# Attention and a gated FFN on one core: the list that sets the order of all steps, replaced

## The chip, the core and the metric

The kernel runs on one NeuronCore of a Trainium2 chip. Its engines are TensorE (PE for its matmuls, PEld for its weight loads), VectorE (DVE), ScalarE (ACT), GpSimd (POOL) and SyncE (SP), whose queue issues the DMAs here. The metric is the device time of one launch in microseconds; lower is better.

## The reference

```python
# q, k, v: (8 batches, 8 heads, 576 positions, 64)
scores = scale * np.matmul(q, k.transpose(0, 1, 3, 2))
rel = pos[:, None] - pos[None, :]
mask_plain = (rel >= 0) & (rel < 32)
mask_dil = (rel >= 0) & (rel < 128) & (rel % 4 == 0)       # heads 4 to 7
attn = softmax(np.where(masks, scores, -1e9))
x = np.matmul(attn, v).transpose(0, 2, 1, 3).reshape(4608, 512)
h = x @ w_in                                               # 512 x 2048
g = h * np.tanh(np.log1p(np.exp(np.minimum(h, 20.0))))     # h where h > 20
out = g @ w_out                                            # 2048 x 512
```

Attention looks back over 32 positions, plain in heads 0 to 3 and every fourth position in heads 4 to 7. The FFN is a product, the Mish function and a second product.

## The kernel before

**Units.** The work is cut into 16 units: half of one batch's positions, 288 each. A unit has four head pairs. Pairs 0 and 1 are plain heads (queries in blocks of 96 rows), pairs 2 and 3 are dilated ones (blocks of 72 rows, one for each residue). For units 0 to 3 attention runs in fp32 on TensorE; from unit 4 on q, k and v are split into two fp16 halves, and transposes go by DMA. The FFN of every unit is made of fp16 products with the high and low halves of weights and activations: 192 matmuls of 128 x 288 in each of the two layers.

**Steps.** The kernel is written as small generator functions, one for each step, and a list called ORDER names them one after another. Each appearance of a name runs the function to its next `yield`. So the list sets the order of the instructions on every engine, and an engine takes its instructions in that order. The steps that matter here, with the lines of the profile:

- `ld`, `lv`: DMAs of a unit's q and k, and of its v (L416 to L444).
- `sp`: the score products of a head pair. Two products with the mask `m_fb` come first (L593), then those of q and k (L596). `sc`: the maxima on DVE (L626). `ex`: for unit 0 TensorE subtracts the maxima (L648), then ACT takes the exponentials (L654); other units have them in L661 or L665.
- `tp`: transposes of the probabilities (L715), copied by ACT (L724). `va`: products with v (L738), the denominator on ACT (L752), the division on DVE (L758, L759).
- `tx`: transposes of the attention's result (L786, L789), its high half by ACT (L796), and its low half, for some pairs by TensorE and ACT (L799, L801).
- `pr`: the power-of-two scales of a unit's inputs, which take a maximum over all partitions (L299 to L308, L470).
- Weights: `wl` fetches a piece of w_in or w_out of 1 MB (L322, L324; 16 pieces, four buffers called `raw`), `wm` takes a copy on ACT (L337), `ww` joins the words of the 64-bit numbers on DVE (L380, L382, L383), `ws` sums over partitions on TensorE (L348, L351) and makes a scale from the maximum on DVE (L355 on), `wp` splits the weights into halves on ACT (L392) and DVE (L395). The first digit is the layer, the second a group of 512 columns, the third one of its two pieces.
- `ff`: products of the first layer (L840) and Mish on ACT (L843). `gt`: the gate's halves on ACT (L859) and DVE (L861). `fo`: products of the second layer (L871), the result (L885), and its DMA (L887).
- `kw`: so many products of zeros on TensorE (L900), whose result is never read. `kw16=0` is 16 of them into bank 0.

The number behind `=` is the buffer that a step takes: of the four PSUM banks, each a pair of 2 KB rows, and of a few SBUF buffers. A step that writes a bank waits until the last reader of it is done, and that holds for the products of zeros too.

```python
def keep_warm(n):
    warm = take("b", banks)
    for _ in range(n):
        nc.tensor.matmul(warm[:, 1, 512 - P:], zeros, zeros, start=True, stop=True)
...
for name in ORDER:
    name, _, at = name.partition("=")
    place[:] = [int(at)] if at else []
    ...
    if hasattr(begun[name], "__next__"):
        next(begun[name], None)
```

**Outside the list.** GpSimd makes an identity (`ident`) and the masks (`m_f`, L239 to L248) with its selection instructions at the kernel's start. ACT makes `ident_b`, `m_fb` and `minus` from them (L252, L250, L271), and the first score product reads `ident_b` and `m_fb`.

Of the kernel before, what the change touches and what calls it, by code (L numbers as in the profile page):

```python
# [42 lines left out]
kw10=3 tx0.2 tx0.2 va0.0 va0.0 tx0.3=3 tx0.3 kw16=0 kw7=0 tx0.3 tx0.3 va0.1=0 va0.1 va0.1 sp1.2=1 sc1.2 ex1.1 kw3=3
tp1.1=3 wl0.1.0 wm0.1.0 sp1.0=2 sc1.0 wl0.2.0 wm0.2.0 ww0.2.0 tx0.0=0 tx0.0 kw12=1 tx0.0 tx0.0 ex1.2 ww0.1.0 ww0.1.0
tx0.1=1 tx0.1 kw16=0 kw7=0 tx0.1 tx0.1 wl0.1.1 wm0.1.1 ww0.1.1 wl0.2.1 wm0.2.1 ww0.2.1 tp1.2=0 tp1.2 tp1.1 ld2 sp2.0=1
sc2.0 ex2.0 kw16=0 ws0.1=0 ex1.0 ww0.2.1 ws0.1 wp0.1.0 sp1.3=3 sc1.3 ex1.3 ww0.1.1 wp0.1.1 kw16=1 kw6=1 ws0.2=1 ws0.2
fs0 wp0.2.1 ff0.0=0 ff0.0 ff0.0 ff0.1=2 ff0.1 ff0.1 ff0.6=1 ff0.6 ff0.6 ff0.7=3 wp0.1.0 ww0.2.0 wp0.2.0 ff0.7 ff0.7
gt0.3=0 wp0.1.1 lv1 pr1 kw16=0 kw7=0 pr1=0 pr1 kw6=2 pr1 pr1 va1.1=2 va1.1 va1.1 va1.2=1 va1.2 va1.2 fs1 tp1.3=3 tp1.3
lv2 tp1.0=0 tp1.0 pr2 wl1.2.0 xa1 tx1.1=2 tx1.1 kw4=1 va1.3=1 va1.3 tx1.1 tx1.2=3 va1.0=0 tx1.2 va1.0 va1.0 va1.3
kw2=2 tx1.2 tx1.2 kw11=2 tx1.0=2 tx1.0 wp0.2.0 wl1.3.1 wm1.3.1 gt0.3 sp2.3=0 sc2.3 tx1.0 tx1.0 sp2.1=3 sc2.1 wl1.3.0  # L50
tx1.3=1 tx1.3 kw13=2 tx1.3 tx1.3 ff1.0=2 ff1.0 wp0.2.1 ex2.3 pr2=1 pr2 kw8=0 pr2 pr2 wm1.3.0 ex2.1 ff1.0 kw4=1 ff0.2=1
ff0.2 ff0.2 ww1.3.1 ff1.1=0 ff1.1 ff1.1 ww1.3.1 ww1.3.0 ww1.3.0 ws1.3=3 ws1.3 wm1.2.0 ww1.2.0 ww1.2.0 gt0.0=1 ff0.3=2
gt0.0 wl1.2.1 wm1.2.1 tp2.1=1 tp2.1 wp1.3.1 wp1.3.1 ff0.4=0 ff0.5=3 ff0.5 ff0.5 ff0.4 ff0.4 gt0.2=2 ww1.2.1 ww1.2.1
va2.1=1 va2.1 va2.1 tp2.3=3 tp2.3 ff0.3 xa3 ff0.3 gt0.1=3 gt1.0=4 wl1.1.0 ws1.2=0 ws1.2 wp1.2.1 wp1.2.1 gt1.0 wp1.3.0
wp1.3.0 gt0.2 ff1.2=3 ff1.3=2 ff1.3 ff1.2 ff1.2 ff1.3 gt1.1=5 gt1.1 va2.3=1 wp1.2.0 wp1.2.0 va2.3 ff1.4=0 ff1.4 ff1.4
fs2 ff1.5=3 va2.3 ff1.5 ff1.5 ld3 lv3 sp3.1=2 sc3.1 sp3.0=0 sc3.0 wm1.1.0 wl1.0.1 wm1.0.1 ww1.0.1 gt1.2=6 gt1.2 gt0.1
ff1.6=3 ff1.6 ff1.6 wl1.1.1 wm1.1.1 sp3.2=1 ww1.1.0 tp2.0=2 tp2.0 wl1.0.0 wm1.0.0 ww1.0.0 xa2 tx2.3=0 tx2.3 tx2.3
ww1.0.0 ff1.7=3 ff1.7 ff1.7 gt1.3=7 gt1.3 xa4 fo1.2.0=2 fo1.2.1 fo1.2.2 ww1.1.1 ex3.1 tp3.1=3 tp3.1 ws1.0=0 ws1.0
fo1.2.3 fo1.2.3 fo1.2.3 sc3.2 ex3.2 sp2.2=3 ld4 sc2.2 ex2.2 ww1.1.0 ex3.0 ws1.1=0 fo1.3.0 fo1.3.1 fo1.3.2 fo1.3.3
fo1.3.3 ws1.1 pr4 pr4 sp3.3=1 sc3.3 ex3.3 pr3 lv4 fo0.2.0=0 fo0.2.1 fo0.2.2 fo0.2.3 fo0.2.3 fo0.2.3 pr4 pr4 va2.0=3  # L60
tp2.2=2 tp2.2 va2.0 va2.0 wp1.0.0 wp1.0.0 fo0.3.0 fo0.3.1 fo0.3.2 fo0.3.3 fo0.3.3 pr4=1 ww1.0.1 fo1.3.3 pr4 fo0.3.3
tx2.0=2 va2.2=3 tx2.0 va2.2 tx2.0 pr4 pr4 tp3.0=0 tp3.0 pr3=2 pr3 va2.2 fo0.0.0=1 wp1.0.1 tx2.1=0 tx2.1 pr3 pr3
va3.1=3 va3.1 va3.1 tp3.2=2 tp3.2 fs4 fo0.0.1 tx2.1 tx2.1 wp1.0.1 tx3.1=2 va3.0=3 va3.0 va3.0 tp3.3=0 tp3.3 tx3.1
tx3.1 fo0.0.2 tx2.2=3 tx2.2 va3.3=0 va3.3 va3.3 tx2.2 tx2.2 ff2.0=2 tx3.3=3 tx3.3 ff2.0 ff2.0 tx3.3 tx3.3 fo0.0.3
fo0.0.3 fo0.0.3 ff2.1=0 ff2.1 ff2.1 ww1.1.1 wp1.1.1 wp1.1.1 va3.2=2 va3.2 va3.2 ff2.2=3 ff2.2 ff2.2 ff2.3=0 ff2.3
wp1.1.0 wp1.1.0 fo0.1.0 ol mr pr4 pr4 fo0.1.1 fo0.1.2 gt2.0=1 gt2.0 fo0.1.3 fo0.1.3 pr4 pr4 pr4 ld5 pr4 pr4 lv5 ff2.3
gt2.1=3 gt2.1 pr5 ff2.4=2 ff2.4 ff2.5=3 ff2.5 ff2.5 ff2.4 gt2.2=2 gt2.2 tx3.0=1 tx3.0 tx3.0 ff2.6=0 ff2.6 ff2.6
ff2.7=3 fo0.1.3 tx3.2=2 tx3.2 tx3.2 ff2.7 ff2.7 gt2.3=0 gt2.3 fo2.2.0=0 fo2.2.1 sp4.3=1 sc4.3 sp4.1=2 sc4.1 fo2.0.0=3
fo2.0.1 fo2.0.2 fs3 ff3.0=1 ff3.2=2 ff3.0 ff3.0 fo2.0.3 fo2.0.3 fo2.0.3 pr5 pr5 pr5 pr5=1 fo2.2.2 fo2.2.3 fo2.2.3 pr5
pr5 pr5 fo2.1.0 fo2.1.1 fo2.1.2 fo2.1.3 pr5 pr5 pr5 pr5 pr5 pr5 pr5 ld6 lv6 ff3.2 ff3.2 fo2.2.3 sp5.1=1 sc5.1 fo2.1.3  # L70
fo2.3.0 fo2.3.1 fo2.3.2 fo2.3.3 fo2.3.3 ex4.1 fo2.1.3 pr6 pr6 pr6 pr6 pr6 pr6 fo2.3.3 sp4.2=2 sc4.2 xa6 ex4.3 tp4.3=1
tp4.3 tp4.3=1 sp5.2=1 fo1.0.0=3 fo1.0.1 fo1.0.2 fo1.0.3 fo1.0.3 fo1.0.3 sp4.0=0 sc4.0 ex4.0 tp4.0=2 tp4.0 tp4.0=2
sc5.2 ff3.1=2 ff3.1 ff3.1 gt3.0=1 gt3.0 fo1.1.0 fo1.1.1 fo1.1.2 fo1.1.3 fo1.1.3 fo1.1.3 pr6 pr6 pr6 pr6 pr6 ld7 pr7
ff3.4=0 ff3.5=2 ff3.5 ff3.5 ff3.4 ff3.4 gt3.2=3 gt3.2 ff3.6=1 ff3.6 ff3.6 ff3.7=3 ff3.7 ff3.7 gt3.3=2 gt3.3 va4.0=2
# [884 lines left out]
```

## Time and profile before

| what | us |
|---|---|
| runs of the kernel before | 929.4, 934.27, 936.63 (median 934.27) |
| the profiled execution's own time | 933.42 |
| its span, first to last instruction | 931.6 |
| TensorE busy in the span | 911.0 |
| VectorE, ScalarE, GpSimd busy | 592.3, 541.0, 22.6 |
| products of zeros: number and busy time | 345, 25.7 |
| first-layer and second-layer products: number and busy time | 3072, 387.8 and 3072, 388.3 |

A row of the timeline has the start in us, the duration, the engine, the line, the operation, what it writes and reads, how many instructions are taken together, and in brackets the idle time of its engine just before it with what ended it. A row of the table by stretch has the stretch, its length, the busy time of PE, PEld, DVE, ACT and POOL with their counts, the clock that TensorE was granted (1.00 is full), the share of the DMA engines, and GB/s. A row of waits has the engine and line that waited, for whom, the us in total, how many times, and the longest.

### The profile page before, as it was taken

The numbers are of one execution on the slowest core, as the hardware profiler recorded it, in microseconds if no ns is written. First come the engines' busy times: TensorE is split into PE (matmuls) and PEld (weight loads), VectorE is DVE, ScalarE is ACT, GpSimd is POOL, SyncE is SP. The second block draws the span as 40 slices with busy tenths as digits, with TensorE's granted clock in tenths as the row PEclk, the third lists the DMA queues.
The fourth block names the chain that finished last, engine by engine and source line by source line (L and its number), as shares of the span: only waits on it lengthen the run. The fifth ranks groups of instructions, "written<-read, shape, count | busy, mean of one in ns | idle before, by whom it ended". The sixth has DMA issues, their size and how long they took to land.

```text
span 931.6 us, 21552 instructions
## 1 busy us (share of the span) xinstructions
PE 911.0 (98%) x9285; PEld 735.0 (79%) x9285; DVE 592.3 (64%) x879; ACT 541.0 (58%) x800; POOL 22.6 (2%) x99
## 2 busy tenths in 40 slices
PE   6889999999999999999999999999999999999998
PEld 4778788888778878878878888887888788788776
DVE  2877888647767767786958677766556757422020
ACT  1677785473566576666665676747545656653141
POOL 1000000040000000000000000000000000000000
PEclk6899999999999999999999999999999999999999
DMA  8283293003334344443434423453224432311000
GB/s 272 87 255 95 93 274 87 20 19 93 107 98 81 90 93 66 90 121 90 113 85 97 101 51 80 88 125 81 40 55 74 122 59 55 43 33 40 20 13 26
DMA packets 156558, 82.33 MB, mean 88 GB/s; under 512 B 122960, under 2 KB 152368, under 8 KB 156464
## 3 DMA queue, kind: packets, MB, share of 16 engines
q1 hardware_dynamic: 156464, 80.97, 34.9%
q8 instruction: 72, 1.18, 0.5%
q14 instruction: 22, 0.18, 0.1%
HBM read 49.02 MB, written 9.44 MB: 63 GB/s over the span
## 4 chain that ended last, share of the span: by engine, by line
PE 96%; issue 1%; ACT 1%; DVE 1%; POOL 0%; DVEq 0%; ACTq 0%; POOLq 0%
PE b L871 41%; PE b L840 40%; PE b L596 4%; PE b L744 3%; PE b L900 2%; PE b L738 2%; PE b L648 1%; PE b L715 1%; PE b L593 1%; PE b L351 0%; PE b L348 0%; PE b L786 0%; PE b L799 0%; ACT x L801 0%; PE b L308 0%
## 5 line engine op out<-in xcount | busy, mean ns | idle before, releaser
L871 PE MATMUL b<-g,w 128*128 128x288 f16 x3072 | 388.3, 286 | 0.0
L840 PE MATMUL b<-x,w 128*128 128x288 f16 x3072 | 387.8, 286 | 0.0
L840 PEld LDWEIGHTS <-w 128*128 128x128 f16 x3072 | 297.9, 98 | 75.8 <-issue 0.3
L871 PEld LDWEIGHTS <-w 128*128 128x128 f16 x3072 | 297.2, 98 | 74.9
L843 ACT ACTIVATE hm<-b,fs 128x576 f32<-128x576 f32 x128 | 92.9, 737 | 116.7 <-PE b L840 99.3
L861 DVE SCALAR_TENSOR_TENSOR g<-hm,sg,g 128x1152 f16<-128x1152 f32 x64 | 90.1, 1414 | 108.7 <-ACT g L859 108.7
L885 ACT ACTIVATE y<-b,fo 128x288 f32<-128x288 f32 x60 | 43.1, 722 | 110.1 <-PE b L871 102.7
L859 ACT ACTIVATE g<-hm,sg 128x1152 f16<-128x1152 f32 x64 | 79.8, 1253 | 3.1 <-PE b L871 1.6
L667 ACT ACTIVATE sb<-sb,ln_p 96x704 f32<-96x704 f32 (+3 forms) x48 | 42.2, 886 | 33.9 <-DVE sb L628 33.8
L628 DVE TENSOR_TENSOR sb<-sb,nm 72x576 f32<-72x576 f32 (+4 forms) x60 | 45.3, 754 | 2.1
L626 DVE TENSOR_REDUCE nm<-sb 72x8 f32<-72x576 f32 (+4 forms) x60 | 44.9, 748 | 1.6
L759 DVE TENSOR_TENSOR xs<-b,rec 96x384 f32<-96x384 f32 (+1 forms) x64 | 39.7, 620 | 6.4 <-DVE rec L758 0.5
L705 DVE TENSOR_TENSOR p<-sb,p 96x704 f16<-96x704 f32 (+3 forms) x31 | 27.7, 897 | 15.6 <-ACT p L703 15.4
L758 DVE RECIPROCAL rec<-den 96x6 f32<-96x6 f32 (+1 forms) x64 | 12.0, 188 | 38.5 <-ACT den L754 29.1
L900 PE MATMUL b<-zeros 128*128 128x128 f16 x345 | 25.7, 235 | 8.1 <-ACT pp L724 2.8
L596 PEld LDWEIGHTS <-q 64*72 64x72 f16 (+1 forms) x1008 | 25.7, 116 | 8.1 <-issue 7.4
L620 DVE SCALAR_TENSOR_TENSOR sb<-b,sc,m_d 72x576 f32<-72x576 f32 (+1 forms) x24 | 22.7, 944 | 14.7 <-PE b L596 11.4
L520 DVE TENSOR_TENSOR q<-qn,q 128x288 f16<-128x288 f32 (+1 forms) x36 | 23.4, 701 | 13.3 <-ACT q L511 13.3
L900 PEld LDWEIGHTS <-zeros 128*128 128x128 f16 x345 | 23.6, 107 | 10.5 <-issue 8.0
L620 DVE SCALAR_TENSOR_TENSOR sb<-b,sc,m_r 96x704 f32<-96x704 f32 (+1 forms) x24 | 23.4, 976 | 12.0 <-PE b L596 11.9
L596 PE MATMUL b<-k,q 64*96 64x128 f16 (+3 forms) x1008 | 30.7, 210 | 0.0
L626 DVE TENSOR_REDUCE nm<-b 96x4 f32<-96x512 f32 (+4 forms) x20 | 14.7, 749 | 20.3 <-PE b L596 20.3
(141 smaller groups left out, 837.9 us busy)
## 6 DMA issues: line engine op xcount, KB each, us to landing
qn<-in_qT SPq DMA_DIRECT2D x16, 576.0 KB
out_T<-y SPq DMA_DIRECT2D x64, 144.0 KB
raw<-in_w_in SPq DMA_DIRECT2D x16, 512.0 KB
raw<-in_w_out SPq DMA_DIRECT2D x16, 512.0 KB
vn<-in_v SPq DMA_DIRECT2D x48, 128.0 KB
knd<-in_kdT SPq DMA_DIRECT2D x16, 208.0 KB
vdn<-in_vd SPq DMA_DIRECT2D x32, 104.0 KB
knp<-in_kT SPq DMA_DIRECT2D x8, 320.0 KB
```

Of the source, the lines that this page charges most:

```text
L596: nc.tensor.matmul(o, q, k, start=start, stop=stop, skip_group_check=True)
L620: nc.vector.scalar_tensor_tensor(args[0], args[1], d["sc"][:nq], args[2], ALU.mult, ALU.add)
L626: nc.vector.tensor_reduce(nm[:nq, :, j:j + n], x, axis=AX.X, op=ALU.max, negate=True)
L628: nc.vector.tensor_tensor(blocked(sb, c0, n, w), x, nm[:nq, :, j:j + n].unsqueeze(3).broadcast_to([nq, 2, n, w]), op=ALU.add)
L667: nc.scalar.activation(x, x, AF.Exp, bias=ln_p[:nq])
L840: nc.tensor.matmul(ph[:, h, :HT], w1[j][:, c, wi, k * P:(k + 1) * P], x_of(d, xi, c), start=(n == 0), stop=(n == len(seq) - 1))
L843: nc.scalar.activation(d["m"][j][:, k0:k0 + 2], ph[:, :, :HT], AF.Mish, scale=d["fs"][:, j:j + 1])
L859: nc.scalar.activation(g[:, 0], m, AF.Identity, scale=sg)
L861: nc.vector.scalar_tensor_tensor(g[:, 1], m, sg, g[:, 0], ALU.mult, ALU.subtract)
L871: nc.tensor.matmul(po[:, :HT], w2[:, e, j, wi, k * P:(k + 1) * P], d["g"][j][:, gi, k, :], start=(j == 0 and n == 0), stop=(j == NCH - 1 a ...
L885: nc.scalar.activation(o, src, AF.Identity, scale=fo)
L900: nc.tensor.matmul(warm[:, 1, 512 - P:], zeros, zeros, start=True, stop=True)
```

## The change

The list ORDER is another one; no function is touched. The steps in it are the same, each as often as before, but for the products of zeros: 482 in place of 345. The list has one line more, so every line of the code behind it has a number that is higher by one.

Three stretches of it have another sequence of steps: from the beginning to the first steps of unit 2's first layer, a block that holds the second layer of unit 6 up to the attention of unit 12, and a few names between. All the rest keeps its sequence and has other bank numbers. Its beginning, as a diff:

```diff
-ld0 kw16=0 kw16=0 kw3=0 sp0.1=0 sp0.2=1 sc0.1 sc0.2 sp0.0=2 sc0.0 sp0.3=3 sc0.3 wl0.3.0 wm0.3.0 ex0.2 ww0.3.0 ww0.3.0
...
+wl0.3.0 wl0.0.1 ld0 wm0.3.0 ww0.3.0 ww0.3.0 wm0.0.1 ww0.0.1 ww0.0.1 kw16=0 kw16=0 kw16=0 kw16=0 kw16=0 kw16=0 kw16=0
+kw16=0 kw16=0 kw16=0 kw16=0 kw16=0 kw16=0 kw16=0 kw2=0 sp0.0=0 sc0.0 sp0.1=1 sc0.1 wl0.0.0 wm0.0.0 ww0.0.0 sp0.3=2
...
```

So 226 products of zeros stand ahead of the first score, where 35 stood, and the other 256 stand in 23 groups up to unit 2, where 310 stood in 20.

**The DMAs at the start.** These are SP's first rows, before; `raw` is a piece of w_in, `qn`, `knp` and `knd` are unit 0's q and k, `vn` and `vdn` its v:

```order
L416 DMA qn_127<-in_qT 128x1152
L418 DMA knp_129<-in_kT 128x2x288
L421 DMA knd_131<-in_kdT 128x4x72 x2
L322 DMA raw_215<-in_w_in 128x512 x2
L322 DMA raw_224<-in_w_in 128x512 x2
L442 DMA vn_293<-in_v 128x4x64 x3
L444 DMA vdn_294<-in_vd 72x4x64 x4
```

And now:

```order
L323 DMA raw_127<-in_w_in 128x512 x2
L323 DMA raw_130<-in_w_in 128x512 x2
L417 DMA qn_133<-in_qT 128x1152
L419 DMA knp_135<-in_kT 128x2x288
L422 DMA knd_137<-in_kdT 128x4x72 x2
L323 DMA raw_396<-in_w_in 128x512 x2
L323 DMA raw_411<-in_w_in 128x512 x2
```

Two pieces of the weights went ahead of q and k, and the next two ahead of v.

**ACT and DVE at the start.** ACT's first rows and DVE's, after three memsets, before; `w13` and `w10` are parts of the first layer's weights, `nm` the maxima of scores:

```order
L252 CAST ident_b_96<-ident_74 96x96
L250 ACTIVATE m_fb_94<-m_f_79 96x352
L271 ACTIVATE minus_100<-ident_74 128x128
L337 ACTIVATE w13_105<-raw_215 128x1024
L337 ACTIVATE w13_105<-raw_224 128x1024
L626 TENSOR_REDUCE nm_187<-b0_70 96x2x2
L626 TENSOR_REDUCE nm_190<-b1_71 72x8
L380 TENSOR_SCALAR w13_105<-w13_105 128x1024
```

And now:

```order
L338 ACTIVATE w13_105<-raw_127 128x1024
L253 CAST ident_b_96<-ident_74 96x96
L272 ACTIVATE minus_100<-ident_74 128x128
L338 ACTIVATE w10_102<-raw_130 128x1024
L251 ACTIVATE m_fb_94<-m_f_79 96x352
L381 TENSOR_SCALAR w13_105<-w13_105 128x1024
L383 SCALAR_TENSOR_TENSOR raw_127<-raw_127,w13_105 128x1024
L384 SCALAR_TENSOR_TENSOR raw_127<-raw_127 128x1024
L381 TENSOR_SCALAR w10_102<-w10_102 128x1024
L383 SCALAR_TENSOR_TENSOR raw_130<-raw_130,w10_102 128x1024
L384 SCALAR_TENSOR_TENSOR raw_130<-raw_130 128x1024
L627 TENSOR_REDUCE nm_382<-b0_70 96x2x2
```

ACT copies one piece ahead of `ident_b` and one ahead of `m_fb`; DVE joins the words of both pieces before its first maxima, where it had four pairs' maxima first.

**TensorE between the second sum of weights and unit 0's first `tx`.** Before, with the groups of zeros left out (`pp` are the transposed probabilities, `xs` the attention's result, the 96 x 384 products those of unit 1 with the mask):

```order
L348 MATMUL b2_72<-w10_102,ones_111 128x512
...
L738 MATMUL b3_73<-vdn_294,pp_390 72x65 x8
L715 MATMUL b1_71<-ident_74,sb_354 72x72 x8
...
L738 MATMUL b2_72<-vdn_294,pp_445 72x65 x8
...
L593 MATMUL b1_71<-m_fb_94,ident_b_96 96x384
...
L596 MATMUL b1_71<-knp_428,qn_426 96x128 x6
L786 MATMUL b0_70<-ident_74,xs_472 128x72 x4
```

And now:

```order
L349 MATMUL b1_71<-w10_102,ones_111 128x512
...
L594 MATMUL b3_73<-m_fb_94,ident_b_96 96x384
...
L597 MATMUL b3_73<-knp_571,qn_569 96x128 x6
...
L597 MATMUL b2_72<-knp_571,qn_569 96x128 x6
L739 MATMUL b1_71<-vdn_459,pp_528 72x65 x8
L716 MATMUL b0_70<-ident_74,sb_530 72x72 x8
...
L739 MATMUL b0_70<-vdn_459,pp_642 72x65 x8
...
L787 MATMUL b3_73<-ident_74,xs_622 128x72 x4
```

Two score pairs of unit 1 stand right behind the sum of weights, ahead of unit 0's products with v, where one stood behind them and the other further down.

More of the change, by code (lines that the diff above doesn't have):

```diff
@@ L43 @@
[L43 to L62, printed above, removed]
@@ new lines @@
+wp0.0.1 wp0.3.0 wp0.0.1 ld1 sp1.1=3 sc1.1 sp1.0=2 sc1.0 ex0.0 lv1 wp0.3.1 va0.2=1 kw11=0 tp0.3=0 tp0.3 va0.2 va0.2
+wp0.0.0 wp0.0.0 kw16=0 kw8=0 va0.3=0 va0.3 tp0.0=3 tp0.0 va0.3 ex1.0 wp0.3.1 wl0.1.0 wm0.1.0 ww0.1.0 ww0.1.0 wl0.2.1
+xa0 kw16=3 kw7=3 tx0.2=3 va0.0=1 tx0.2 kw15=2 tp1.0=2 kw16=0 kw10=0 tx0.2 tx0.2 tp1.0 va0.0 va0.0 tx0.3=0 kw13=3
+va0.1=3 va0.1 tx0.3 va0.1 wl0.2.0 kw16=2 kw5=2 tx0.3 wm0.2.0 tx0.3 ex1.1 kw14=2 tx0.1=2 tx0.1 tx0.0=1 sp1.2=3 pr1
+kw11=0 tx0.1 tx0.0 sp1.3=0 tx0.0 ww0.2.0 wl0.1.1 wm0.1.1 tx0.1 wm0.2.1 sc1.2 tx0.0 kw9=2 tp1.1=2 tp1.1 ex1.2 ww0.1.1
```

225 lines of the change are left out of this document (120 added, 105 removed).

## The prediction

> **What bounds the kernel now.** I read the page first, then the table of busy time by stretches of 20 us, then TensorE's waits, then the timeline of the first 101 us.
>
> ```profile
> PE 911.0 (98%) x9285; PEld 735.0 (79%) x9285; DVE 592.3 (64%) x879; ACT 541.0 (58%) x800; POOL 22.6 (2%) x99
> 0.00:20.00 20.00, 10.86 (x87) 8.39 (x89) 2.66 (x8) 4.38 (x6) 2.85 (x17) 0.71 0.83 253
> 20.00:40.00 20.00, 18.23 (x166) 14.17 (x165) 15.50 (x24) 8.82 (x13) 0.00 (x0) 0.78 0.34 119
> 40.00:60.00 20.00, 17.50 (x243) 15.43 (x242) 15.43 (x29) 13.61 (x23) 0.24 (x2) 1.00 0.77 264
> 60.00:80.00 20.00, 18.55 (x182) 14.38 (x180) 19.20 (x29) 17.24 (x35) 0.00 (x0) 1.00 0.57 145
> 80.00:100.00 20.00, 18.00 (x221) 15.42 (x220) 12.83 (x30) 13.64 (x28) 0.27 (x3) 1.00 0.37 124
> 100.00:120.00 20.00, 19.92 (x192) 16.78 (x192) 18.77 (x33) 15.83 (x25) 0.00 (x0) 1.00 0.27 88
> 120.00:140.00 20.00, 20.00 (x191) 15.84 (x190) 16.78 (x25) 15.64 (x24) 0.00 (x0) 1.00 0.88 259
> ```
>
> The columns after the stretch are busy us of PE, PEld, DVE, ACT and POOL, then TensorE's granted clock. From 120 us on TensorE is always busy, to 920 us. So its remaining work sets the end, and no order of it can gain there. All that can be won lies in the first 120 us: 16.9 us of idle TensorE (9.1, 1.8, 2.5, 1.4, 2.0 and 0.1), the products of zeros, and work at half clock. The same views show where:
>
> ```profile
> 1.05 3.92 PE L900 MATMUL b<-zeros 128*128 128x128 f16 x35 [1.05 <-DVE zeros L895]
> 8.00:9.00 1.00, 0.00 (x0) 0.00 (x0) 0.00 (x0) 0.00 (x0) 0.00 (x0) 0.76 1.02 386
> 10.83 0.28 POOL masks.py:199 TENSOR_SCALAR_AFFINE_SELECT ident<-ident 128x128 f32<-128x128 f32 x1 [9.57 <-issue]
> 11.14 0.27 ACT L252 CAST ident_b<-ident 96x96 bf16<-96x96 f32 x1 [9.13 <-POOL ident masks.py:199]
> 12.91 0.29 ACT L271 ACTIVATE minus<-ident 128x128 f16<-128x128 f32 x1
> 13.05 0.74 PE L593 MATMUL b<-m_fb,ident_b 96*96 96x352 bf16 x2 [8.09 <-ACT m_fb L250]
> 13.11 1.10 ACT L337 ACTIVATE w<-raw 128x1024 f32<-128x1024 f32 x1
> 14.73 1.12 ACT L337 ACTIVATE w<-raw 128x1024 f32<-128x1024 f32 x1 [0.52 <-DMA raw<-in_w_in]
> 15.27 0.95 DVE L626 TENSOR_REDUCE nm<-b 96x4 f32<-96x512 f32 x2 [14.28 <-PE b L596]
> 13.05:25.45 12.40, 12.39 (x76) 8.21 (x76) 7.01 (x10) 2.29 (x3) 0.00 (x0) 0.50 0.89 290
> 26.29 3.89 PE L900 MATMUL b<-zeros 128*128 128x128 f16 x44 [0.84 <-ACT sb L654]
> 28.00:29.00 1.00, 1.00 (x12) 1.00 (x10) 0.02 (x1) 1.00 (x3) 0.00 (x0) 0.50 0.00 0
> 29.00:30.00 1.00, 1.00 (x21) 1.00 (x19) 0.00 (x0) 1.00 (x3) 0.00 (x0) 1.00 0.00 0
> 68.63 1.63 PE L840 MATMUL b<-x,w 128*128 128x288 f16 x12
> ```
>
> GpSimd's first selection comes at 10.83 us. The mask follows, and the first score stands until 13.05. The 35 zeros ended at 4.97, the clock fell at about 8.5, and the first scores, 12.4 us of them, ran at half clock; it rose at 29.0, 2.7 us after 44 zeros began. DVE has nothing to do until 15.3. The first product of the FFN comes at 68.63.
>
> **The change, part by part.** *Start.* 226 products of zeros stand ahead of the first score instead of 35, and two 1 MB pieces of w_in are fetched ahead of unit 0's q and k. A zero product takes 3.92/35 = 112 ns at half clock. At full clock these rows give the prices:
>
> ```profile
> 31.95 2.17 PE L900 MATMUL b<-zeros 128*128 128x128 f16 x36 [0.86 <-DVE wm L355]
> 20.91 4.54 PE L648 MATMUL b<-nm,ident 72*72 72x288 f32 x12
> 34.06 2.35 PE L648 MATMUL b<-nm,ident 96*96 96x256 f32 x12
> 46.27 0.49 PE L593 MATMUL b<-m_fb,ident_b 96*96 96x384 bf16 x2
> 46.69 0.90 PE L596 MATMUL b<-knp,qn 64*96 64x128 f32 x12
> 13.73 1.49 PE L596 MATMUL b<-knp,qn 64*96 64x128 f32 x12
> ```
>
> A zero product: (2.17 less 0.1 for the last one's pipeline)/36 = 58 ns. When the clock rises is not shown for zeros that go on, only bounded: no sooner than 2.7 us, no later than twice the 3.92 us in which 35 did not raise it. I take 4.0 us: 36 at 112 ns, 190 at 58 ns for 11.0 us, so the first score starts at 1.05 + 4.0 + 11.0 = 16.1 (bounds 15.4 and 17.9). It is 3.05 us later than now.
>
> The Trainium skill, "TensorE: Matmul & The Clock Gate", Part 1, says that the clock doubles after a busy window of about 3.4 us that runs free of the kernel, so 3.4 to 6.8 us after the start; by it the first score would come between 15.8 and 17.4 us. The two steps of the trace, 8.5 and 29.0, are six such windows apart.
>
> Is anything else later than 16.1? In today's order 3.2 MB (q, k and two pieces) have landed by 14.73, where ACT waited for the second piece. The new order fetches the same four items in another sequence, so q and k are there by about 14.7. ACT copies the first piece before GpSimd is done, then ident_b at 11.14, minus, and the second piece until 12.85; the mask is ready at 13.4. DVE's three word operations take 3.2 us a piece:
>
> ```profile
> 21.70 0.68 DVE L380 TENSOR_SCALAR w<-w 128x1024 int32<-128x1024 int32 x1
> 22.41 1.23 DVE L382 SCALAR_TENSOR_TENSOR raw<-raw,w 128x1024 int32<-128x1024 int32 x1
> 23.67 1.23 DVE L383 SCALAR_TENSOR_TENSOR raw<-raw 128x1024 int32<-128x1024 int32 x1
> 31.20 0.69 DVE L355 TENSOR_REDUCE wm<-b 128x1 f32<-128x512 f32 x1 [3.18 <-PE b L348]
> 39.07 0.68 DVE L355 TENSOR_REDUCE wm<-b 128x1 f32<-128x512 f32 x1
> ```
>
> The second piece's words end at 12.85 + 3.2 = 16.0, just before DVE's first score. So 6.4 us of DVE work move into time in which DVE had none. If ACT's copies were late, each us would hold the first reduction as long.
>
> *Full clock.* The four score pairs cost 12.4 us with the first six rows of L648 at half clock. At full clock they cost 2 x 1.25 (0.35 to the products, 0.90 for them), 2 x 1.1 for the pairs of 72 rows (estimated down from those) and 2.35: 7.1 us. That saves 5.3. The 44 zeros at 88 ns would have cost 58: 1.3 more.
>
> *Zeros after the first score.* 310 now, 482 - 226 = 256 then: 54 fewer at 58 ns, 3.1 us. They stand in 23 groups where 20 stood, as the gaps are shorter.
>
> *Idle time after the first score.* 16.9 - 9.1 = 7.8 us now. In the new order I went along the engines by hand with the durations above. TensorE: scores to 20.7, the three subtractions to 24.0, the first piece group's sums to 25.1. DVE takes their maxima from 25.6 (now 31.20), and the second group's from about 31.3 (now 39.07). There the gain is largest. It shrinks after that, because the transposes of unit 0 hang on a chain through ACT. Up to the first FFN product both orders hold the same TensorE work (tp1.0 stands for tp1.2). Now: 68.63 - 13.05 = 55.6, less 5.7 idle, 239 zeros (13.9, and the 1.3) and 5.3 for the clock, 29.4 us. Then: 16.1 + 29.4 + 213 zeros (12.4) = 57.9 and the idle time. By hand I find 1.9 of it, at three waits of zeros for ACT, and put 1.5 for handing over between engines: first FFN product at 61.3, 7.3 us earlier. From there to the last zeros I find three more waits of about 0.8 us, again on ACT, and add 1.2: 7.0 in all, 0.8 less than now. Bounds: 2 (only the hand-overs) and 15 (twice today's).
>
> *After that.* Steps of units 7 to 12 are reordered too, in the stretch 500 to 740, where TensorE is busy all the time. No gain is possible there. From each transpose to its first reader, and from each gate to its first reader, the new order leaves as much TensorE work as the tightest place of today's, which waits for nothing. I price it at 0, and at 3 us if one such place per unit waits 0.5. DVE and ACT, at 507.9 and 467.5 us of 811.6, cover it.
>
> ```profile
> 120.00:931.60 811.60, 807.92 (x8208) 650.44 (x8206) 507.94 (x732) 467.46 (x673) 19.18 (x77) 1.00 0.33 77
> ```
>
> **Sum.** +3.05 - 5.3 - 1.3 - 3.1 - 0.8 = -7.45, so -7.5 us. The profiled execution took 933.4 (span 931.6 and 1.8 around it): 925.9. The median of the runs, 934.27, is 0.85 above it: 926.8.
>
> **The rivals.**
>
> *Every gap closes.* The search laid zeros into shorter gaps; if its durations hold, idle time falls to 2 or less instead of 7: 5 us more, 921.8. For it: 23 groups of zeros, each fitted to a gap. Against it: today's order was fitted too, and waits all the same:
>
> ```profile
> PE b L900 <- ACT pp L724: 2.8, 2, 1.5
> PE b L900 <- ACT sb L661: 0.9, 1, 0.9
> PE b L900 <- ACT x L801: 0.9, 2, 0.6
> ```
>
> *The clock falls again.* From 16.1 to 25.1 only two zeros stand in TensorE's list; the rest is scores and fp32 subtractions. Just that work, 12.4 us of it without a pause, did not raise the clock between 13.05 and 25.45. If it does not hold it either, the clock falls 3.5 us in, as it did 3.5 us after 4.97. The 5.5 us left take twice as long, and the next 39 zeros cost 3.6 in place of 2.3: 6.8 us, 933.6. Against it: from 37.1 to 45.1 TensorE had, beside fp32 work and 1.4 us of idle time, only these zeros, one more and four sums of about 1.1 us, and the table by stretch has the clock at 1.00 there:
>
> ```profile
> 40.57 1.11 PE L900 MATMUL b<-zeros 128*128 128x128 f16 x17
> ```
>
> The same page of the Trainium skill, in Part 4, says that transpose mode does not count as busy for this gate; no run here shows whether fp32 products do.
>
> *Zeros behind late banks* (the other side). The first zero of a group waits until ACT or DVE has read the bank it writes, and then all of them run, though real work may be ready. A wait there costs its length and saves no zeros. Today these waits are 7 us in 20 groups, 0.35 each. From 0.62 us a group (14.4 in all) the gain is gone. At 1.5 us, the longest of the three rows, in half of the groups the idle time is 17.3 and hand-overs 1.5 more: 11.8 above my 7.0, 938.6; in three quarters of them, 947.
>
> *The later reordering waits*: 3 us less, 929.8.
>
> **How the numbers follow.** Forecast 0.44, every gap closes 0.27, clock falls 0.12, zeros behind late banks 0.11, later waits 0.06. About 1% (9.3 us) is what a measurement of this kernel can tell from no change; runs of it lie from 929.4 to 936.63. Faster by over 1%, below 924.9: most of the second case (0.23) and the lower end of the forecast, with idle time under 5 us (0.12): 0.35. Slower by over 1%, above 943.6: the late banks from about 0.95 us a group on (16.8 above my 7.0 is 23.8 in all), 0.05. Between: 0.60. The range takes in the forecast with its bounds of idle time and clock, the closed gaps to 919, and the fallen clock to 935.
>
> **What would show it.** Right: first score near 16 us with the clock at 1.00 up to the first FFN product; DVE's first maxima at L355 (one line further down) near 25.6; first FFN product near 61; idle TensorE after the first score near 7 us, and none after 120. Wrong: a clock of 0.50 between 20 and 29; a first score after 18; waits in front of zeros above 14 us; idle TensorE between 500 and 740.

## The result, and the profile after

The changed kernel takes 921.75 us (median of four runs, 921.26 to 923.0), the kernel before, in the same set of runs, 934.18 (929.4 to 936.63). The ratio is 0.9875, with a 95% interval of [0.9834, 0.9916]: 0.8 to 1.7% less time. The forecast was 926.8. By the profiled executions the span went from 931.6 to 921.1 us, 10.5 less, where 7.45 were forecast. One execution of a later kernel, 1167.8 us at a mean granted clock of 0.751 where its five others took 914.65 to 918.01, is left out of that kernel's figures.

This is the changed kernel's table by stretch, with the columns of the table before (busy us of PE, PEld, DVE, ACT and POOL, the granted clock, the DMA share, GB/s):

```profile
0.00:20.00 20.00, 18.96 (x276) 17.73 (x278) 8.89 (x14) 6.49 (x8) 2.85 (x17) 1.00 0.93 299
20.00:40.00 20.00, 18.65 (x215) 15.04 (x216) 17.88 (x35) 12.41 (x21) 0.00 (x0) 1.00 0.73 197
40.00:60.00 20.00, 19.12 (x255) 16.22 (x255) 16.09 (x29) 15.54 (x34) 0.24 (x2) 1.00 0.73 224
60.00:80.00 20.00, 19.46 (x200) 16.61 (x198) 15.46 (x30) 13.68 (x28) 0.27 (x3) 1.00 0.19 60
80.00:100.00 20.00, 18.72 (x191) 15.07 (x191) 16.83 (x31) 15.01 (x26) 0.00 (x0) 1.00 0.66 213
100.00:120.00 20.00, 20.00 (x191) 16.11 (x190) 18.80 (x28) 15.04 (x25) 0.00 (x0) 1.00 0.45 125
```

Idle TensorE is 1.04 us at the start and 1.35 + 0.88 + 0.54 + 1.28 = 4.05 us after the first score, where 7.8 stood. From 100 us on there is none. The clock column reads 1.00 in every stretch, where 0.71 and 0.78 stood in the first two; how far its first microseconds can be read comes further down.

The next rows are its timeline; they answer to the rows of before, and the third shows the last 24 of the 226 zeros:

```profile
12.47 0.28 POOL masks.py:199 TENSOR_SCALAR_AFFINE_SELECT ident<-ident 128x128 f32<-128x128 f32 x1 [11.21 <-issue]
14.21 0.48 ACT L251 ACTIVATE m_fb<-m_f 96x352 bf16<-96x352 f32 x1
14.79 1.50 PE L901 MATMUL b<-zeros 128*128 128x128 f16 x24
16.13 0.46 PE L594 MATMUL b<-m_fb,ident_b 96*96 96x352 bf16 x2
20.58 3.40 PE L649 MATMUL b<-nm,ident 96*96 96x256 f32 x16
25.16 0.68 DVE L356 TENSOR_REDUCE wm<-b 128x1 f32<-128x512 f32 x1
30.98 0.69 DVE L356 TENSOR_REDUCE wm<-b 128x1 f32<-128x512 f32 x1 [0.29 <-PE b L349]
59.27 7.51 PE L841 MATMUL b<-x,w 128*128 128x288 f16 x60
84.57 10.45 PE L841 MATMUL b<-x,w 128*128 128x288 f16 x84
```

The first score starts at 16.13, 3.1 us later than before, yet DVE's first maxima come at 25.16 in place of 31.20 and the first FFN product at 59.27 in place of 68.63. So 9.4 of the 10.5 us had come by then. GpSimd's first selection came 1.6 us later (12.47, not 10.83; the last section comes back to it), and TensorE did not wait for it, since the zeros ran longer. Here are all of TensorE's waits:

```profile
PE b L901 <- ACT pp L725: 2.1, 3, 0.8
PE b L901 <- ACT x L802: 1.5, 2, 0.9
PE b L901 <- DVE zeros L896: 1.0, 1, 1.0
PE b L901 <- ACT hm L844: 0.4, 1, 0.4
```

In these rows the engine and line that waited come first, then for whom, us in total, times, and the longest. All four have L901 in front: apart from the start, every wait that is left stands ahead of a product of zeros (4.0 us in six places), and none ahead of work. The second half of the experiments starts from that.

### The profile page after: what moved, and what is told of

Read it like the earlier page. It is cut to its first block, busy times and chain, and to the rows that moved or that the text cites. A ratio compares the mean times of both kernels' runs of the same rounds, so it can differ in the third digit from the quotient of the medians.

```text
span 921.1 us, 21816 instructions
## 1 busy us (share of the span) xinstructions
PE 911.5 (99%) x9422; PEld 738.0 (80%) x9422; DVE 593.1 (64%) x879; ACT 545.5 (59%) x804; POOL 22.0 (2%) x99
## 4 chain that ended last, share of the span: by engine, by line
PE 99%; ACT 1%; issue 0%; DVE 0%; ACTq 0%
PE b L872 41%; PE b L841 41%; PE b L597 4%; PE b L745 3%; PE b L901 3%; PE b L739 2%; PE b L716 1%; PE b L594 1%; PE b L649 0%; PE b L352 0%; PE b L349 0%; PE b L800 0%; PE b L787 0%; ACT pp L725 0%; PE b L309 0%; ACT x L802 0%
## 5 line engine op out<-in xcount | busy, mean ns | idle before, releaser
L760 DVE TENSOR_TENSOR xs<-b,rec 72x512 f32<-72x512 f32 (+1 forms) x64 | 39.7, 620 | 6.5 <-DVE rec L759 0.5
L901 PE MATMUL b<-zeros 128*128 128x128 f16 x482 | 33.4, 229 | 5.1 <-ACT pp L725 2.1
L901 PEld LDWEIGHTS <-zeros 128*128 128x128 f16 x482 | 31.0, 103 | 7.3 <-issue 5.0
L759 DVE RECIPROCAL rec<-den 72x8 f32<-72x8 f32 (+1 forms) x64 | 12.0, 188 | 36.2 <-ACT den L755 27.3
L597 PEld LDWEIGHTS <-q 64*72 64x72 f16 (+1 forms) x1008 | 25.8, 116 | 8.3 <-issue 7.6
L597 PE MATMUL b<-k,q 64*72 64x72 f16 (+3 forms) x1008 | 30.9, 210 | 0.0
```

What stands on the lines that cost most here:

```text
L597: nc.tensor.matmul(o, q, k, start=start, stop=stop, skip_group_check=True)
```

## The experiments

The theory after the result: the time is that of TensorE's list up to about 100 us. The start pays through two things, the warm clock and DVE's early words, which both set when the first maxima come; the rest comes from the zeros and the waits between 30 and 100 us. The rival: one of the two does it all, or the reordering of units 7 to 12 takes part. The kernel before had a median of 934.84, 934.22 and 934.59 us beside the three sets of runs that follow.

### The first part of the list alone

The new list up to the second layer of unit 2, and from there the list of before; the banks and gate buffers of the first part are renumbered so that the two fit. Of the block in which the two lists differ, one place:

```diff
-pr10 pr10 pr10 tx8.0=0 ex9.0 tp9.0=0 tp9.0 tp9.0=2 fo6.3.2 fo6.3.3
+pr10 pr10 pr10 pr10 ex9.2 tp9.2=0 tp9.2 ex9.0 tp9.0=2 tp9.0 tp9.0=2 pr10 ld11 pr11 pr11 fo6.3.2 fo6.3.3
```

> The new order up to the middle of the feed-forward of unit 2 (all zeros lie in this part), and from there the old order, so without the new order of units 7 to 12; banks and gate buffers of the first part are renumbered so that they fit. Theory: TensorE is busy all the time from 100 us on in both profiles, so only the first part pays: within 1 us of the whole change, 920.8 to 922.8, ratio to the kernel before 0.986 to 0.988. Rival: the later reordering brought the 3 us by which the forecast (925.9 for the profiled execution, 921.1 + 1.8 measured) was missed: about 925, ratio 0.990.

Measured: 922.12 us (921.29 to 923.16), ratio to before 0.9873 [0.9851, 0.9895], the same as the whole change. In both kernels TensorE is busy throughout that stretch, first the whole change, then this one:

```profile
500.00:740.00 240.00, 240.00 (x2509) 193.19 (x2508) 157.24 (x222) 149.91 (x213) 4.56 (x28) 1.00 0.38 82
```

```profile
500.00:740.00 240.00, 240.00 (x2531) 193.59 (x2530) 159.48 (x226) 150.04 (x217) 5.48 (x29) 1.00 0.37 81
```

The later reordering is worth nothing that can be measured.

### The cold start in the new order

```diff
-kw16=0 kw16=0 kw16=0 kw16=0 kw16=0 kw16=0 kw16=0 kw16=0 kw16=0 kw16=0 kw16=0 kw16=0 kw16=0 kw16=0 kw2=0 sp0.0=0
+kw16=0 kw16=0 kw3=0 sp0.0=0
```

> The changed kernel with 35 products of zeros ahead of the first score in place of 226, all else as in the change. Theory (the warm clock pays more than the early start): the first score comes at about 14.7 us, when the mask is ready, the scores and subtractions, 7.7 us in the changed kernel (16.1 to 23.8), run at half clock for 12 to 13 us and end at 27.2, 3.4 later, and the next zeros run at half clock until it rises, 1 to 2 us more: 4.5 to 5.5 us slower than the change, 926 to 927. Rival (the early words of the second weight piece are what pays, DVE cannot take a score before 17.6 us anyway, and later gaps swallow the rest): within 1.5 us of the change, 921 to 923.

Measured: 928.06 us (922.83 to 928.78), ratio to before 0.9923 [0.9895, 0.995]: 5.9 us slower than the run above, a little over what the theory gave. Two of the six executions, 922.83 and 925.3, lost only 0.7 and 3.2, see the last section; the profile is that of the slowest. Its timeline, and the stretch of the scores:

```profile
14.96 0.75 PE L594 MATMUL b<-m_fb,ident_b 96*96 96x352 bf16 x2 [10.12 <-ACT m_fb L251]
22.82 6.50 PE L649 MATMUL b<-nm,ident 96*96 96x256 f32 x16
31.36 0.69 DVE L356 TENSOR_REDUCE wm<-b 128x1 f32<-128x512 f32 x1 [3.88 <-PE b L349]
65.88 7.51 PE L841 MATMUL b<-x,w 128*128 128x288 f16 x60
```

```profile
14.96:29.53 14.57, 14.57 (x82) 9.45 (x83) 9.81 (x13) 5.10 (x7) 0.00 (x0) 0.50 0.92 241
```

The subtractions of L649 take 6.50 us where they took 3.40, and DVE, done with its words, sits idle 3.88 us before the first maxima. The half clock sets the pace here.

### The warm start in the old order

```diff
-ld0 kw16=0 kw16=0 kw3=0 sp0.1=0
+ld0 kw16=0 kw16=0 kw16=0 kw16=0 kw16=0 kw16=0 kw16=0 kw16=0 kw16=0 kw16=0 kw16=0 kw16=0 kw16=0 kw16=0 kw2=0 sp0.1=0
```

> The kernel before with 226 products of zeros ahead of the first score in place of 35, all else as before. Theory: scores and subtractions end at about 24.0 in place of 25.45, the 44 zeros after them cost 1.3 us less, but DVE still has the weight words of two pieces behind the scores, so that its first maxima at L355 come only some 1.5 us sooner than 31.2 and most of the gaps after them stay: 1.5 to 4 us faster than before, about 931.5. Rival A (the clock is the whole gain): the first maxima come near 26 and the time is 922 to 925. Rival B (the start 3 us later is not won back, since DVE sets the pace after the scores): 934 to 937.

Measured: 930.84 us (929.79 to 932.01), ratio 0.9973 [0.9953, 0.9993], 4.0 us faster than before; both rivals are out.

```profile
27.32 0.68 DVE L355 TENSOR_REDUCE wm<-b 128x1 f32<-128x512 f32 x1
64.75 11.92 PE L840 MATMUL b<-x,w 128*128 128x288 f16 x96
```

The first maxima come 3.9 us sooner than before, not the 1.5 that the expectation put, and the first FFN product 3.9 sooner: the shift is handed on whole.

### DVE's words late in the new order

```diff
-wm0.3.0 ww0.3.0 ww0.3.0 wm0.0.1 ww0.0.1 ww0.0.1 kw16=0
+wm0.3.0 wm0.0.1 kw16=0
...
-sc0.3 ex0.3
+sc0.3 ww0.3.0 ww0.3.0 ww0.0.1 ww0.0.1 ex0.3
```

> The changed kernel with DVE's words of the first two weight pieces (six operations, 6.3 us) put back behind the reductions of the last score, as they stood before; fetches, ACT's copies, the 226 zeros and all else as in the change. Theory: DVE's work before the first maxima at L356 grows by 6.3 us, so these come at 31 in place of 25.2, near the 31.2 of the kernel before, and the first FFN product at about 64: 4 to 6 us slower than the change, 926 to 928. Rival (DVE has room after 25 us, and the clock and the zeros alone are the gain): within 1.5 us of the change, 921 to 923.5.

Measured: 929.44 us (927.47 to 930.11), ratio 0.9949 [0.9929, 0.9968], 7.7 us slower than the change and 1.4 above the theory's range. The theory had the maxima right and the first FFN product 2 us too early:

```profile
28.98 1.01 PE L349 MATMUL b<-w,ones 128*128 128x512 bf16 x2 [4.47 <-DVE w L381]
31.36 0.68 DVE L356 TENSOR_REDUCE wm<-b 128x1 f32<-128x512 f32 x1
65.98 7.51 PE L841 MATMUL b<-x,w 128*128 128x288 f16 x60
```

```profile
26.00:30.00 4.00, 1.02 (x4) 0.46 (x4) 3.93 (x4) 0.00 (x0) 0.00 (x0) 0.58 1.10 200
30.00:34.00 4.00, 4.00 (x43) 4.00 (x42) 2.70 (x8) 1.29 (x2) 0.00 (x0) 0.57 0.13 31
```

TensorE stood 4.47 us at the sums of L349 for DVE's words, and the clock fell in that wait, so the zeros behind it ran at half clock as well.

### Both undone

```diff
-wm0.3.0 ww0.3.0 ww0.3.0 wm0.0.1 ww0.0.1 ww0.0.1 kw16=0 kw16=0 kw16=0 kw16=0 kw16=0 kw16=0 kw16=0 kw16=0 kw16=0 kw16=0 kw16=0 kw16=0 kw16=0 kw16=0 kw2=0
+wm0.3.0 wm0.0.1 kw16=0 kw16=0 kw3=0
...
-sc0.3 ex0.3
+sc0.3 ww0.3.0 ww0.3.0 ww0.0.1 ww0.0.1 ex0.3
```

> The changed kernel with both undone at once: 35 products of zeros ahead of the first score in place of 226, and DVE's words of the first two weight pieces behind the last score's reduction; the rest of the order as in the change. Theory (the two overlap): each alone brought the first maxima at L356 from 25.2 to 31.4 us and the first FFN product from 59.3 to 65.9, and both together cost less than their sum: the scores end at half clock, DVE's last score reduction ends near 24.3 in place of 22.0, 3.1 + 6.3 us of words follow, and the first maxima come at about 33.8: 2.4 us later than with one undone, 930.5 to 932.5. Rival (they add, 6.1 and 7.5 us on 921.9): 935 to 936.5.

Measured: 930.81 us (929.18 to 932.75), ratio 0.998 [0.9958, 1.0001]. Against the 921.75 of the change the two cost 6.3 and 7.7 us when undone alone, together 9.1: they overlap and do not add. The theory had the time, but its step to the maxima (33.8, where the profile has 32.22) is not tested by the profile, which is of the fastest of the twelve executions (929.18): there the clock rose during the scores, see the last section.

```profile
32.22 0.68 DVE L356 TENSOR_REDUCE wm<-b 128x1 f32<-128x512 f32 x1
66.31 7.51 PE L841 MATMUL b<-x,w 128*128 128x288 f16 x60
```

The rows also show what the rest of the new list brings. From the first maxima to the first FFN product it takes 34.1 us, here (32.22 to 66.31) as in the change (25.16 to 59.27). The old list takes 37.4, in the kernel before (31.20 to 68.63) as with the warm start (27.32 to 64.75). So the 10.5 us of the profiles are 6.0 up to the first maxima, 3.3 from there to the first FFN product, and 1.1 behind it.

### No zeros behind the first score

All 256 out; the 226 ahead of it stay.

```diff
-ww0.3.1 ww0.3.1 kw2=1 ws0.3=1 ws0.3 lv0 pr0 pr0 kw16=3 kw16=3 kw7=3 pr0=3
+ww0.3.1 ww0.3.1 ws0.3=1 ws0.3 lv0 pr0 pr0 pr0=3
```

> The changed kernel without the 256 products of zeros that stand behind the first score; the 226 ahead of it stay. Theory A (these zeros keep the clock up): the clock falls to 0.50 at some place between 25 and 60 us, the work of these 33 us without the zeros, about 21 us, takes up to twice as long, of which idle time covers part: 5 to 12 us slower than the change, 927 to 934. Theory B (fp32 and the other products hold the clock alone): the clock stays at 1.00, the zeros' time becomes idle time, and the waits of zeros for a bank (4 us in six places) are gone where real work was ready: 918.5 to 922.

Measured: 920.56 us (916.42 to 923.22), ratio 0.9848 [0.9819, 0.9877]: not slower than the change. Neither theory held whole. The clock did fall, twice (0.50 from about 27 to 34 us and from 41 to 58), as in these rows:

```profile
28.00:29.00 1.00, 1.00 (x5) 0.71 (x5) 0.97 (x2) 1.00 (x3) 0.00 (x0) 0.50 0.73 138
56.00:57.00 1.00, 1.00 (x9) 0.84 (x6) 1.00 (x2) 0.38 (x1) 0.00 (x0) 0.50 0.16 38
```

```profile
60.75 7.51 PE L841 MATMUL b<-x,w 128*128 128x288 f16 x60
83.88 10.45 PE L841 MATMUL b<-x,w 128*128 128x288 f16 x84 [0.24 <-ACT x L802]
```

The first FFN product came 1.5 us later than in the change, but the long piece of 84 products behind it 0.7 earlier. As I read it, some of the zeros earn their time, through the clock, and others cost it. The next four runs look for the second kind.

### Without the last nine groups, and without three more

The first kernel drops the 43 zeros behind the first FFN product (the last two of them stand at 160 us), the second also the groups of 24, 23 and 13 that waited for ACT.

```diff
-wp0.0.0 wp0.0.0 kw16=0 kw8=0 va0.3=0
+wp0.0.0 wp0.0.0 va0.3=0
...
-wl0.2.1 xa0 kw16=3 kw7=3 tx0.2=3
+wl0.2.1 xa0 tx0.2=3
...
-tx0.3=0 kw13=3 va0.1=3
+tx0.3=0 va0.1=3
...
-tp2.0=0 tp2.0 kw2=3 tx1.0=3
+tp2.0=0 tp2.0 tx1.0=3
```

> The changed kernel without the last nine groups of zeros, 43 products, which stand between the first FFN product and about 100 us; the 213 zeros of the other groups stay. Theory, from the run without any zeros behind the first score, where the piece that begins at 99.42 us in the changed kernel began at 98.23 though its first FFN product came 1.5 us later (60.75 against 59.27): these groups stand on the path, since each first waits for a bank that ACT still reads and then runs ahead of work that is ready, and they cost 2.7 us: 918.8 to 919.8. Rival: they only fill idle time, or the clock needs them: 921.5 to 924.

> As the last one, and without three more groups of zeros: those of 24, 23 and 13 products that begin at 36.39, 40.25 and 46.90 us in the changed kernel, each behind a wait for ACT. Theory: the work behind each is held up for the zeros' own time, 1.3, 1.3 and 0.7 us, and the idle time that comes instead does not bring the clock down, since 153 zeros stay between the first score and the FFN: 2 to 3.3 us faster than the run without the last nine groups, 916 to 917.5. Rival: DVE and ACT set the pace there (zeros hide), or the clock falls: the same as the last one or slower, 919 or more.

Measured: 919.13 us (918.49 to 919.34), ratio 0.984 [0.9817, 0.9862], and 916.4 us (915.86 to 917.98), ratio 0.9814 [0.9791, 0.9837]. Both came where the theory had them. From the first kernel, the piece of 84 products, 2.2 us earlier than in the change although the first FFN product came at the same time (59.24):

```profile
82.38 10.45 PE L841 MATMUL b<-x,w 128*128 128x288 f16 x84 [0.24 <-ACT x L802]
```

From the second:

```profile
36.39 1.25 PE L739 MATMUL b<-vdn,pp 72*72 72x65 f32 x16 [0.78 <-ACT pp L725]
38.97 0.47 PE L787 MATMUL b<-ident,xs 72*128 72x72 f32 x4 [0.83 <-ACT pp L725]
56.30 7.51 PE L841 MATMUL b<-x,w 128*128 128x288 f16 x60
```

In the change these were the places of zeros:

```profile
36.39 1.50 PE L901 MATMUL b<-zeros 128*128 128x128 f16 x24 [0.78 <-ACT pp L725]
40.25 1.45 PE L901 MATMUL b<-zeros 128*128 128x128 f16 x23 [0.82 <-ACT pp L725]
```

The idle time is the same, 0.78 us, and ends with the same copy by ACT at 36.39. But there 24 zeros followed it, and the products with v (L739), which that very copy had released, came at 37.73. The zeros filled no gap: they stood behind it.

### Fewer zeros still

The first kernel takes six more groups out and shortens two; the second takes out two and shortens one.

```diff
-kw16=3 kw16=3 kw7=3 pr0=3
+kw16=3 kw16=3 kw1=3 pr0=3
...
-tx0.2 kw15=2 tp1.0=2 kw16=0 kw10=0 tx0.2
+tx0.2 tp1.0=2 kw13=0 tx0.2
```

> As the run with twelve groups taken out (the last nine, and those of 24, 23 and 13), and with fewer zeros again: the groups of 11, 15, 14, 11, 9 and 4 are out, 26 become 13, 39 become 33. 70 zeros stay between the first score and the first FFN product. Theory A (in the run without any zeros behind the first score TensorE waited for nothing at these places, so the zeros hold up ready work as the others did): about 3 us of zeros less, of which half reaches the first FFN product: 914 to 915.5. Theory B (they cover waits for ACT and DVE, which now become idle time, and the clock falls once between 40 and 57 us as it did without any): 916 to 920.

> As the run with twelve groups taken out, and without the groups of 15 and 14 as well, with 33 zeros in place of 39 ahead of unit 0's maximum. Theory A (these zeros hold up ready work): up to 1.9 us of zeros less, 914.5 to 916. Theory B (they cover waits): no change, 916 to 917.5; a clock that falls would show as 918 or more.

Measured: 915.21 us (915.09 to 916.6), ratio 0.9813 [0.978, 0.9845], and 915.82 us (914.65 to 918.01), ratio 0.9817 [0.9784, 0.9851]. The second cannot be told from the run of 916.4. In the first both theories hold in part: its first FFN product comes at 55.07 in place of 56.30, though the clock fell once more:

```profile
38.00:40.00 2.00, 1.54 (x11) 1.54 (x11) 1.90 (x4) 2.00 (x9) 0.00 (x0) 0.50 0.98 342
55.07 7.51 PE L841 MATMUL b<-x,w 128*128 128x288 f16 x60
```

These are the fastest versions tried, some 6 us under the change and 19 under the kernel before. Between them lies no difference that the runs show.

### An earlier start

On the run of 916.4, with 30 zeros fewer at the start and two steps of DVE's words moved, one behind the last score's reduction and one behind DVE's first maxima:

```diff
-kw16=0 kw16=0 kw16=0 kw16=0 kw16=0 kw16=0 kw16=0 kw16=0 kw16=0 kw16=0 kw16=0 kw16=0 kw16=0 kw16=0 kw2=0
+kw16=0 kw16=0 kw16=0 kw16=0 kw16=0 kw16=0 kw16=0 kw16=0 kw16=0 kw16=0 kw16=0 kw16=0 kw4=0
...
-wm0.0.0 ww0.0.0 sp0.3=2
+wm0.0.0 sp0.3=2
...
-sc0.3 ex0.3 ww0.3.1 ww0.3.1 kw2=1 ws0.3=1 ws0.3
+sc0.3 ww0.0.0 ex0.3 ww0.3.1 kw2=1 ws0.3=1 ws0.3 ww0.3.1
```

> As the run without the last nine groups and the three of 24, 23 and 13, and with an earlier start: 196 zeros in place of 226 ahead of the first score, and two steps of DVE (the first word operation of the fourth piece, the other two of the third) put behind the last score's reduction and behind the first maxima, where nothing waits for them at once. Theory: the mask is ready at 14.7 us, the first score starts at 14.8 in place of 16.1, the first maxima come 1.3 us earlier, and most of that reaches the end: 1 us faster than without these moves, 915 to 916.5. Rival: DVE, busy with the second piece's words to 17.7, holds the scores' reductions, and its moved words come back later: no faster than without these moves.

Measured: 920.9 us (918.97 to 922.41), ratio 0.9858 [0.9834, 0.9882]: 4.5 us slower than without the moves. The theory failed in both its steps:

```profile
15.67 0.46 PE L594 MATMUL b<-m_fb,ident_b 96*96 96x352 bf16 x2 [1.99 <-ACT m_fb L251]
28.82 0.15 DVE L467 TENSOR_TENSOR m<-m 72x1 f32<-72x1 f32 x1
29.03 0.27 PE L300 MATMUL b<-ident,m 128*1 128x128 f32 x1 [1.93 <-DVE m L467]
82.84 12.07 PE L841 MATMUL b<-x,w 128*128 128x288 f16 x84 [0.24 <-ACT x L802]
```

The mask came later in this execution (GpSimd's first selection at 13.41 us), so the scores began 0.5 us earlier and not 1.3, after 2 us of idle TensorE. And the moved words stood ahead of L467, a 0.15 us operation on which TensorE's next product and all scales of unit 0 hang; it came at 28.82, where it stood at 26.52 in the change. The theory asked who waits for the moved steps, and not who stands behind them on DVE. This is not the whole loss. The span of this profile is 5.0 us longer than that of the run without the moves (919.6 against 914.6), and L300 stands only 2.0 later (29.03 against 27.00). The other 3.0 go with a clock that fell twice, to 0.50 from about 42 to 45 us and from about 83 to 86: 1.4 us more up to the first FFN product, and 1.6 in the 84 products (12.07 in place of 10.45). Why it fell here and not without the moves, no run shows.

### The late zeros of the kernel before

```diff
-pr1 kw16=0 kw7=0 pr1=0 pr1 kw6=2 pr1
+pr1 pr1=0 pr1 pr1
```

and so for all eight groups behind its first FFN product (71 zeros).

> The kernel before without its last eight groups of zeros, 71 products (4 us), which stand behind the first FFN product; all else as before. Theory: as in the changed kernel, part of them stand ahead of work that is ready or behind a bank that comes late; of their 4.0 us and the 1.2 us of waits in front of them about half is given back: 931 to 933. Rival: they fill waits of unit 1 for ACT and DVE, which become idle time: within 1 us of the kernel before.

Measured: 931.82 us (926.7 to 933.0), ratio 0.9972 [0.995, 0.9994], 2.8 us faster than before: the theory. Ten of the twelve executions lie between 931.28 and 933.0. Its first FFN product came 1.15 us later than in the profile of before, and its piece of 48 products 1.57 earlier:

```profile
98.73 6.04 PE L840 MATMUL b<-x,w 128*128 128x288 f16 x48 [0.25 <-DVE m L470]
```

So the old list lost time to its zeros in the same way, and part of what the change won there, it could have had by leaving zeros out.

## Why the prediction was right, and where it missed

The direction, the place and the mechanism were right; the size was 2.9 us too small by the profile (925.9 forecast for an execution that took 923.0). By the medians it was 5.05 (926.8 against 921.75): the forecast put the median 0.85 above the profiled execution, and that of the change lies 1.25 below it. These 2.1 us are the spread of executions, and no step of the sum.

**Start.** Forecast 16.1, measured 16.13, out of two errors that cancel. The last 24 zeros take from 14.79 to 16.13, 56 ns each, not 58. With 112 and 56 ns, 226 zeros that end at about 16.2 put the rise of the clock at 6.0 us, 5.0 after the first zero and not 4.0. The rows by 1 us agree; a product counts in each row that it touches:

```profile
5.00:6.00 1.00, 1.00 (x12) 1.00 (x11) 0.00 (x0) 0.00 (x0) 0.00 (x0) 1.00 1.08 328
7.00:8.00 1.00, 1.00 (x22) 1.00 (x20) 0.00 (x0) 0.99 (x2) 0.00 (x0) 1.00 1.02 385
```

The clock column says 1.00 in both, so at the very start the clock is to be read from the durations. The moment is not fixed: in the nine profiles with 226 zeros ahead, the first score starts between 15.82 and 16.51, which by the same prices is an estimated rise 4.2 to 5.6 us after the first zero. The Trainium skill, "TensorE: Matmul & The Clock Gate", Part 1, has a busy window of about 3.4 us that runs free of the kernel. By it an estimate of the rise is 3.4 to 6.8 us after the first zero, and the trace agrees. The mask was ready at 14.69, not 13.4, and the second piece's words ended at 17.7, not 16.0. The prediction took over GpSimd's first selection from the old order, and in the new one it comes later. The first reduction waited some 0.2 us for the words (it starts at 17.64, and at 17.38 where the words are late), which was gone again at the maxima:

```profile
17.64 1.94 DVE L627 TENSOR_REDUCE nm<-b 96x4 f32<-96x512 f32 x4
```

**Full clock.** Scores and subtractions were to end at 24.0 and ended at 23.8, the first sums at 25.1 and 24.99, the maxima at 25.6 and 31.3, where 25.16 and 30.98 were measured. The warm start in the old order measures the two terms: the scores and subtractions took 6.85 us (15.83 to 22.68) in place of 12.40, and the 44 zeros 2.62 in place of 3.89, so 5.55 and 1.27 where 5.3 and 1.3 were put. What the sum did not see is how the terms hang together. The later start, -5.3 and -1.3 make 3.55 us net for the warm start; in the old order it measured 4.0. But in the new order it is worth 6, since there the scores began at 14.96 even with 35 zeros. DVE's early words are worth 7.7. With either one undone the first maxima come at 31.4. I had priced them as if each stood by itself, and the words only through the idle time that they would save.

**Zeros after the first score.** 54 fewer, 3.1 us: right in number and price (54 at 56 ns are 3.0).

**Idle time after the first score: this step failed.** I forecast 7.0, and 4.05 were measured; the 2.95 us between are the whole miss by the profile, but for 0.1. The waits that I found by hand were right, three of 1.9 in all before the FFN and three more of about 2.4 behind it: measured 0.78 + 0.82 + 0.62 and 0.52 + 0.41 + 0.89. What was wrong are the 1.5 and 1.2 us that I put on top "for handing over between engines": all idle time stands at these six waits, and hand-overs added none. As I read it, the durations that I walked along already held the hand-over, and where TensorE is ahead of its next input, zeros fill the difference.

**After that.** Priced at 0, and the run with the first part alone shows 0.

**The rivals.** *Every gap closes* had the number (921.8) but not the mechanism: 4 us of gaps stayed, at the places found by hand. *The clock falls again* is out for the change: it held from 16 to 25 us with two zeros, four sums and else fp32 work. *Zeros behind late banks*, which I gave 0.11 as a loss against before, is at work in the change all the same: six of its groups wait 4.0 us, as those of before waited 7, and removing twelve groups, six of them these, gave back 5.4 us. It did not turn the sign; the old list had the same fault. My words for it, that all zeros of a group run behind the wait, "though real work may be ready", were the most useful of the prediction, and I used them only to price a loss, not to ask what both lists could win.

## What to carry to other kernels

Filler work that waits for the same release as the real work behind it does not fill the gap but follows it, and its whole length is lost: read each wait in front of filler, and ask what else that release set free. Two changes that set the same moment (here the first maxima, through the clock and through DVE's list) are not to be priced one by one; undo each alone and both together. And when durations are walked along engine by engine, a surcharge for hand-overs needs a row that shows it; here there was none.

## What the hardware showed that I had not expected

**The clock depends on the execution.** The run with both undone and the cold start have the same 35 zeros and then the same scores from about 14.9 us on. In the profile of the first, the products of L597 took 1.49 us for the first pairs, and from 19.68 us on they ran at full clock, with no zeros since 5 us. Its clock column reads 1.00 up to 29 us, so this too is read from the durations:

```profile
17.70 1.49 PE L597 MATMUL b<-knp,qn 64*96 64x128 f32 x12
19.68 0.74 PE L597 MATMUL b<-knd,qn 64*72 64x72 f32 x16
```

In the cold start's profile the same products took

```profile
19.86 1.24 PE L597 MATMUL b<-knd,qn 64*72 64x72 f32 x16
```

and the clock read 0.50 through 14.57 us of busy TensorE. So these scores can raise the clock, and do not always: the prediction took it from one execution that such work "did not raise the clock". By the Trainium skill, the same page and part, the gate's window runs free of the kernel, so that the moment varies from run to run. The same section of the Trainium skill states that one busy window lifts the clock. The cold start's profile does not agree, since by its busy time four such windows (14.57 / 3.4) passed at 0.50.

The spreads fit two ways of the clock. The cold start's six runs lie over 6.0 us (922.83 to 928.78), the warm start in the old order's twelve over 2.2. Of 52 executions of the kernel before, 11 lie between 928.0 and 930.8 and 41 between 932.9 and 937.6, with none between. The mean granted clock of each execution is on record. Of the 41 slower ones 29 read 0.985 to 0.989, of the 11 faster ones 8 read 0.994. By an estimate, 0.988 and 0.994 of some 931 us are 22 and 11 us at half clock, and the profile of before, at 0.988, has it from 8.5 to 29.0. The other 15 read 0.998 or more, which says little, as the column of both undone shows. In the cold start 922.83 us goes with 0.994, 925.3 with 0.990, and 928.2 to 928.8 with 0.986 and 0.987; the sixth, 927.9, reads 0.999. None of the faster executions of the kernel before was profiled, so this stays a reading of the means.

**Keeping the clock up cost as much as letting it fall.** Without any zeros behind the first score TensorE worked at half clock for some 21.4 us between 27 and 58 us, and so lost about 10.7 us. The 213 zeros that were left out there had taken 11.9 (213 at 56 ns). The faster lists lie between. That of 916.4 us keeps 153 of these zeros, and its clock reads 1.00; that of 915.21 keeps 70, and its clock fell once.

**GpSimd's first selection comes later in the new order.** It starts at 9.78, 10.83 and 11.16 us in the three profiles with the old start of the list, and between 12.23 and 13.41 in the eleven with the new one. Within one order it moves by 1.2 to 1.4 us. What in the new order delays it, the weights that are fetched first for instance, no run separates. A start that is planned to the mask's last half microsecond, as in the attempt at an earlier one, has to allow for both.
